# Converting the last weight matrix by column halves, with conversion slots in every chain

## The chip, the cores and the metric

The kernel runs on one core of one Trainium2 chip. The metric is device microseconds (us) of one execution, the median of several runs. Five engines work side by side from their own in-order queues: TensorE (PE: matmuls and transposes; PEld: its weight loads), VectorE (DVE), ScalarE (ACT), GpSimd (POOL) and SyncE (SP), which here issues every DMA.

## What the reference computes

Causal attention with 2 x 12 heads over 448 positions of 64, then two gated layers over the 896 tokens of width 768. Cut to what matters:

```python
x = attn_out.transpose(0, 2, 1, 3).reshape(896, 768)
h = x @ moe_w_in                      # 768 -> 2048
x = (h * sigmoid(h)) @ moe_w_out      # 2048 -> 768
h = x @ moe2_w_in                     # 768 -> 1024
sm = exp(h - max(h)) / (sum(exp(h - max(h))) + 1e-9)
solu = h * sm
ln = (solu - mean(solu)) / sqrt(var(solu) + 1e-6) * moe2_g_ln
out = ln @ moe2_w_out                 # 1024 -> 768
```

The inputs are float32, except that the four weight matrices reach the chip as 64-bit floats, as pairs of 32-bit words.

## The kernel before, in words

The work has five stages: attention, then the four matrix products. Every product is done with operands split into a high and a low part (`h`, `l`), and three matmuls for each block: high by high, high by low, low by high. So each weight chunk has to be loaded, converted from 64-bit words to float32 with integer operations, and split.

A chunk is 128 rows by 384 columns. `order` (lines 238 to 245) lists all chunks of the four matrices in the order in which they are loaded and converted; the sixteen chunks of the last one, `(4, 0)` to `(4, 15)`, stand at its end. `RAWS` = 4 loads are ahead of the conversion. For one chunk the steps are: `load_w` (L193, a DMA issued by SyncE), `conv_a` (L202, ScalarE scales the high words), `shift_w` (L217, VectorE shifts the low words), `conv_b` (L209 and L212, VectorE joins the words; between the two it shifts the next chunk), and the split. For the last matrix the split is `split4`: `high4` (L496, ScalarE: `w4h` = chunk times the gain) and `low4` (L500, VectorE: `w4l` = chunk times the gain minus `w4h`).

The stage around the change is the last one, lines 481 to 615. The 896 tokens are seven tiles of 128 (`NT` = 7). For each tile `t` there is

- `gemm3(t)` (L535 to L537): the third product, 2 x 512 columns in the PSUM tile `h`, 36 matmuls;
- `chain(t)` (L544 to L562): the softmax-like gate and the layer norm's statistics, alternating between VectorE and ScalarE. VectorE takes the maximum (L549), ScalarE the exponential (L550), VectorE divides and multiplies (L552 to L555), ScalarE squares (L557, "Square") and subtracts the mean (L558, "Identity"), VectorE and GpSimd finish (L559, L560). It has two places, `fill` and `fill2`, in which other work is put in the queues;
- `transp4(t)` (L570): eight TensorE transposes into the PSUM tiles `tp`;
- `evict4(t)` (L578 on ScalarE, L579 on VectorE): splits the transposed tile into `lh` and `ll`;
- `gemm4(t)` (L590 to L592): the fourth product. It goes over the output columns in two halves, 0 to 383 and 384 to 767 (0 to 511 and 512 to 767 for the last tile), each with its own PSUM buffer of the pool `gm`, which has two. For each half it goes over eight row blocks `k` with three matmuls each. ScalarE then evicts the half (L593) and SyncE writes it out (L594).

Everything is in a hand-written order: each engine's queue follows the order of the program's text. The loop of lines 602 to 609 does `gemm3(t)` and `chain(t)` for the seven tiles. From tile 5 on it also puts `transp4(0)` and `transp4(1)` ahead of the chain, and the chain's first place is then taken by `evict4(0)` and `evict4(1)`. The loop of lines 611 to 615 does `gemm4(t)` and, behind it, `transp4(t + 2)` and `evict4(t + 2)`.

The conversions of the last matrix are put in slots. One slot is a call of `feed4` (L508): it takes the oldest waiting chunk, issues `high4` for it, `conv_b` for the next one of the list if there is any, `low4` for the first, then `conv_a` of the one after and a load. With three chunks waiting, as at the first slot, it splits one more. There is one slot before chain 0, two in each of chains 0 to 4, and one in each of chains 5 and 6 (the second place; the first has the eviction). What is left is done by `feed_to(4, N4 - 1)` at line 610, behind chain 6.

Before the change chunk `m` holds row block `k = m // 2` and column half `n = m % 2` of the last matrix (lines 490 and 649).

Of the kernel before, what the change touches and what calls it, by code (L numbers as in the profile page):

```python
# [20 lines left out]
DM = H * D  # L21
# [4 lines left out]
KF2 = DF2 // 128  # L26
NT = T // 128
CH = 384
# [14 lines left out]
def fused(ctx, tc, qT, kT, vv, vt, w1, w2, w3, w4, gl, out):  # L43
# [18 lines left out]
    with tc.manual_schedule():  # L62
# [174 lines left out]
        N4 = KF2 * DM // CH  # L237
# [9 lines left out]
        pend = []  # L247
# [11 lines left out]
        def feed():  # L259
            m = fed[0]  # L260
            fed[0] += 1
            at = lambda a: order[a] if a < len(order) else None
            if m + 1 < len(order):
                conv_a(*order[m + 1])
            for _ in range(2):
                if len(pend) >= lag[0]:
                    finish(pend.pop(0))
            if m < len(order):
                n, c = order[m]
                conv_b(n, c, x3 if n == 3 else xs, at(m + 1))  # L270
                pend.append(m)
            if m + RAWS < len(order):
                load_w(*order[m + RAWS])

        def feed_to(n, c):
            while (n, c) not in ready:
                feed()
# [3 lines left out]
        def pair():  # L281
            t = psd.tile([128, B, 512], F32, name="h", tag="h")
            return [t[:, b] for b in range(B)]
# [49 lines left out]
        for i in range(NP2 + TL + 2):  # L333
            live = i < NP2
            n, r, p, x = i - 1, i - TL, i - TL - 1, i - TL - 2
# [61 lines left out]
        for f in range(KF):  # L397
            t = pair()
# [3 lines left out]
            for half in range(2):  # L402
# [3 lines left out]
                m = 2 * f + half + 4  # L406
# [80 lines left out]
        nc.sync.dma_start(gain, gl)  # L487

        def part4(m):
            k, n = divmod(m, 2)  # L490
            sl = slice(CH * n, CH * n + CH)
            return wx[4, m], gain[:, k:k + 1], w4h[:, k, sl], w4l[:, k, sl]

        def high4(m):
            x, g, h, _ = part4(m)
            nc.scalar.activation(h, x, AF.Copy, scale=g)  # L496

        def low4(m):
            x, g, h, l = part4(m)
            nc.vector.scalar_tensor_tensor(l, x, g, h.bitcast(F32), ALU.mult, ALU.subtract)  # L500
            wx.pop((4, m))
            ready.add((4, m))
# [5 lines left out]
        def feed4():  # L508
            m = fed[0]
            fed[0] += 1  # L510
            if len(pend) >= XS:
                split4(order[pend.pop(0)][1])
            old = order[pend.pop(0)][1] if pend else None
            if old is not None:
                high4(old)
            if m < len(order):
                conv_b(*order[m], xs, order[m + 1] if m + 1 < len(order) else None)
                pend.append(m)
            if old is not None:
                low4(old)  # L520
            if m + 1 < len(order):
                conv_a(*order[m + 1])
            if m + RAWS < len(order):
                load_w(*order[m + RAWS])
# [3 lines left out]
        def gemm3(t):  # L528
            ps = psd.tile([128, 2, 512], F32, name="h", tag="h")
            ts = slice(128 * t, 128 * t + 128)  # L530
            for n in range(2):
                for k in range(KD):
                    o = (n * KD + k) * 512
                    wh, wl = w3h[:, o:o + 512], w3l[:, o:o + 512]
                    nc.tensor.matmul(ps[:, n], yh[:, k, ts], wh, start=k == 0, stop=False)  # L535
                    nc.tensor.matmul(ps[:, n], yh[:, k, ts], wl, start=False, stop=False)  # L536
                    nc.tensor.matmul(ps[:, n], yl[:, k, ts], wh, start=False, stop=k == KD - 1)  # L537
            hps[t] = ps
# [5 lines left out]
        def chain(t, fill, fill2):  # L544
            ps = hps[t]
            s = dp.tile([128, 12], F32, name="s", tag="s", bufs=LAG + 2)
            e = dp.tile([128, 2, 512], F32, name="e", tag="e", bufs=LAG)
            col = lambda m: s[:, m:m + 1]
            nc.vector.tensor_reduce(col(0), ps, AX.XY, ALU.max, negate=True)  # L549
            nc.scalar.activation(e, ps, AF.Exp, bias=col(0), accum_out=col(1))  # L550
            fill()
            nc.vector.tensor_scalar(col(2), col(1), 1e-9, None, ALU.add)  # L552
            nc.vector.reciprocal(col(3), col(2))
            nc.vector.scalar_tensor_tensor(e, e, col(3), ps, ALU.mult, ALU.mult, accum_out=col(4))
            nc.vector.tensor_scalar(col(5), col(4), -1.0 / DF2, None, ALU.mult)  # L555
            fill2()
            nc.scalar.activation(ps, e, AF.Square, bias=col(5), accum_out=col(6))  # L557
            nc.scalar.activation(e, e, AF.Identity, bias=col(5))  # L558
            nc.vector.tensor_scalar(col(7), col(6), 1.0 / DF2, 1e-6, ALU.mult, ALU.add)  # L559
            nc.gpsimd.tensor_tensor(col(9), col(7), mhalf, ALU.pow)  # L560
            lns[t] = e
            rstd[t] = col(9)  # L562
# [3 lines left out]
        def transp4(t):  # L566
            for n in range(2):
                tp = tps[t, n] = psd.tile([128, 4, 128], F32, name="tp", tag="tp")
                for m in range(4):
                    nc.tensor.transpose(tp[:, m], lns[t][:, n, 128 * m:128 * m + 128], ident)  # L570

        def evict4(t):
            lh = dp.tile([128, KF2, 128], F32R, name="lh", tag="lh")
            ll = dp.tile([128, KF2, 128], F32R, name="ll", tag="ll")
            for n in range(2):
                tp = tps.pop((t, n))
                sl = slice(4 * n, 4 * n + 4)
                nc.scalar.activation(lh[:, sl], tp, AF.Copy)  # L578
                nc.vector.tensor_tensor(ll[:, sl], tp, lh[:, sl].bitcast(F32), ALU.subtract)  # L579
            lnt[t] = (lh, ll)  # L580
# [17 lines left out]
        def fill():  # L598
            if pend or fed[0] < len(order):
                feed4()  # L600

        for t in range(NT):
            gemm3(t)
            if t == 0:
                fill()
            z = t - NT + 2
            if z >= 0:
                transp4(z)
            chain(t, (lambda: evict4(z)) if z >= 0 else fill, fill)
        feed_to(4, N4 - 1)  # L610
        for t in range(NT):
            gemm4(t)
            if t + 2 < NT:
# [48 lines left out]
```

## Time and profile before

| what | value |
|---|---|
| three runs | 462.68, 465.28, 465.45 us; median 465.28 |
| the profiled execution, its own time | 463.06 us |
| its span from first to last instruction | 461.3 us |
| TensorE busy in the span | 444.8 us, 96% |
| VectorE, ScalarE, GpSimd busy | 322.3, 231.4, 152.9 us |
| granted TensorE clock, mean | 0.993 |

A span is measured from the first to the last instruction; what lies around it (1.76 us here) belongs to the execution's time. Busy time of TensorE is modelled from pipelined matmuls: a matmul's own duration overlaps the next one's, so distances are read from start to start. The granted clock is the share of full speed (2.4 GHz) that TensorE was given: 1.00 or 0.50, and a value between them is a stretch with both.

### The profile page before, as it was taken

What the parts mean: (1) busy time and instruction counts of PE and PEld (TensorE: products, weight loads), DVE (VectorE), ACT (ScalarE), POOL (GpSimd) and SP (SyncE); (2) the same over time, 40 slices, a digit from 0 to 9 for tenths busy, and PEclk for the clock granted to TensorE, in tenths of its full rate; (3) what the DMA queues carried; (4) which work ended last, traced back from release to release, by engine and by line L of the source; (5) the groups of instructions that cost most, each with busy time, mean ns of one, the idle gap of its engine ahead of it and who ended that gap; (6) DMA issues with size and microseconds to landing.
All of it is one profiled execution on the core that took longest, in us unless ns stands there. A gap on an engine that the chain in (4) does not pass through costs nothing.

```text
span 461.3 us, 6916 instructions
## 1 busy us (share of the span) xinstructions
PE 444.8 (96%) x2360; PEld 380.5 (82%) x2360; DVE 322.3 (70%) x720; ACT 231.4 (50%) x538; POOL 152.9 (33%) x156
## 2 busy tenths in 40 slices
PE   8899999999999999999999999999999998799997
PEld 5555555778999999999999999999888887699996
DVE  4977989759999898887695968846797767221110
ACT  4999899644433434344444334434466665321211
POOL 2312315527777566674332333323400000000000
PEclk9999999999999999999999999999999999799999
DMA  5776211204433424333754847544033300010111
GB/s 159 219 240 177 65 35 36 78 25 137 138 103 104 135 74 133 103 104 106 218 161 134 234 149 220 175 112 136 2 103 104 91 11 1 17 53 34 49 38 51
DMA packets 26386, 49.20 MB, mean 107 GB/s; under 512 B 6128, under 2 KB 13936, under 8 KB 26352
## 3 DMA queue, kind: packets, MB, share of 16 engines
q1 hardware_dynamic: 26352, 48.77, 35.7%
q8 instruction: 18, 0.29, 0.3%
q14 instruction: 16, 0.13, 0.1%
HBM read 46.01 MB, written 2.75 MB: 106 GB/s over the span
## 4 chain that ended last, share of the span: by engine, by line
PE 84%; DVE 8%; ACT 6%; issue 1%; DVEq 0%; ACTq 0%
PE h L290 7%; PE h L292 7%; PE h L291 7%; PE h L423 7%; PE h L422 7%; PE h L424 7%; PE h L537 4%; PE ps L590 4%; PE h L536 4%; PE h L535 4%; PE ps L591 4%; PE ps L592 4%; PE pv L175 4%; ACT e L126 3%; DVE e L120 3%; PE tr L149 3%
## 5 line engine op out<-in xcount | busy, mean ns | idle before, releaser
L228 POOL TENSOR_TENSOR wl<-wx,wh 128x384 fp32r<-128x384 f32 x64 | 74.7, 1168 | 100.2 <-ACT wh L227 99.0
L227 ACT ACTIVATE wh<-wx 128x384 fp32r<-128x384 f32 x64 | 33.4, 523 | 71.6 <-DVE wx L212 29.8
L202 ACT ACTIVATE wr<-wr 128x384 f32<-128x384 f32 x91 | 49.9, 554 | 33.3 <-DMA wr<-w_in 33.3
L290 PE MATMUL h<-xh,wh 128*128 128x448 f32 x180 | 65.8, 366 | 0.7 <-DVE sg L298 0.7
L212 DVE SCALAR_TENSOR_TENSOR wx<-wr,wx 128x384 uint32<-128x384 uint32 x96 | 66.4, 692 | 0.0
L291 PE MATMUL h<-xl,wh 128*128 128x448 f32 x180 | 65.7, 365 | 0.0
L292 PE MATMUL h<-xh,wl 128*128 128x448 f32 x180 | 65.7, 365 | 0.0
L217 DVE TENSOR_SCALAR wr<-wr 128x384 uint32<-128x384 uint32 x96 | 57.9, 603 | 4.0 <-DMA wr<-w_in 3.8
L209 DVE SCALAR_TENSOR_TENSOR wx<-wr 128x384 uint32<-128x384 uint32 x96 | 59.1, 615 | 1.3 <-POOL gl L300 1.3
L422 PE MATMUL h<-gh,wh 128*128 128x448 f32 x160 | 58.6, 367 | 0.0
L423 PE MATMUL h<-gl,wh 128*128 128x448 f32 x160 | 58.6, 366 | 0.0
L424 PE MATMUL h<-gh,wl 128*128 128x448 f32 x160 | 58.6, 366 | 0.0
L300 POOL TENSOR_TENSOR gl<-sg,gh 128x448 fp32r<-128x448 f32 x32 | 41.0, 1280 | 20.8 <-DVE gh L299 11.0
L126 ACT ACTIVATE e<-e,st 128x384 f32<-128x384 f32 (+3 forms) x84 | 43.3, 526 | 5.5 <-DVE st L120 5.5
L590 PE MATMUL ps<-w4h,lh 128*128 128x384 f32 (+2 forms) x112 | 39.4, 352 | 4.5 <-ACT w4h L496 4.5
L579 DVE TENSOR_TENSOR ll<-tp,lh 128x512 fp32r<-128x512 f32 x14 | 9.0, 686 | 43.4 <-ACT lh L578 43.4
L591 PE MATMUL ps<-w4l,lh 128*128 128x384 f32 (+2 forms) x112 | 38.9, 347 | 0.0
L592 PE MATMUL ps<-w4h,ll 128*128 128x384 f32 (+2 forms) x112 | 38.7, 346 | 0.0
L290 PEld LDWEIGHTS h<-xh,wh 128*128 128x128 f32 x180 | 33.8, 188 | 3.8 <-DVE sg L298 1.1
L136 POOL TENSOR_TENSOR e<-e,st 128x384 f32<-128x384 f32 x24 | 19.6, 838 | 50.1 <-ACT aT L164 34.7
L291 PEld LDWEIGHTS h<-xl,wh 128*128 128x128 f32 x180 | 33.8, 188 | 2.7
L292 PEld LDWEIGHTS h<-xh,wl 128*128 128x128 f32 x180 | 33.8, 188 | 2.7
(101 smaller groups left out, 849.8 us busy)
## 6 DMA issues: line engine op xcount, KB each, us to landing
wr<-w_in SPq DMA_DIRECT2D x96, 384.0 KB, 3.7
k<-kT_in SPq DMA_DIRECT2D x12, 224.0 KB, 3.2
q<-qT_in SPq DMA_DIRECT2D x12, 192.0 KB, 3.3
v<-vv_in SPq DMA_DIRECT2D x12, 192.0 KB, 2.9
out<-o SPq DMA_DIRECT2D x12, 192.0 KB, 1.8
qt<-qT_in SPq DMA_DIRECT2D x24, 16.0 KB, 2.8
v<-vt_in SPq DMA_DIRECT2D x12, 32.0 KB, 2.5
out<-o SPq DMA_DIRECT2D x1, 256.0 KB, 2.0
```

What stands on the lines that cost most here:

```text
L209: nc.vector.scalar_tensor_tensor(xu, high, 0x80000000, low, ALU.bitwise_and, ALU.bitwise_or)
L212: nc.vector.scalar_tensor_tensor(xu, high, 3, xu, ALU.logical_shift_left, ALU.bitwise_or)
L217: nc.vector.tensor_scalar(low, low, 29, None, ALU.logical_shift_right)
L228: (lo_engine or nc.gpsimd).tensor_tensor(l, x, h.bitcast(F32), ALU.subtract)
L290: nc.tensor.matmul(ps[:, :S], wh, rh, start=k == 0, stop=False)
L291: nc.tensor.matmul(ps[:, :S], wh, rl, start=False, stop=False)
L292: nc.tensor.matmul(ps[:, :S], wl, rh, start=False, stop=k == KD - 1)
L422: nc.tensor.matmul(ps[:, :S], wh, rh, start=f == 0, stop=False)
L423: nc.tensor.matmul(ps[:, :S], wh, rl, start=False, stop=False)
L424: nc.tensor.matmul(ps[:, :S], wl, rh, start=False, stop=f == KF - 1)
L590: nc.tensor.matmul(ps[:, :w], lh[:, k], w4h[:, k, ns], start=k == 0, stop=False)
L591: nc.tensor.matmul(ps[:, :w], lh[:, k], w4l[:, k, ns], start=False, stop=False)
```

## The change

The last matrix is laid out and converted by column halves: chunk `m` now holds row block `m % 8` of column half `m // 8`. In the chains of the last two tiles a slot is added behind the eviction in the first place, and the remainder behind the last chain becomes a loop over slots.

```diff
         def part4(m):
-            k, n = divmod(m, 2)
+            n, k = divmod(m, KF2)
             sl = slice(CH * n, CH * n + CH)
             return wx[4, m], gain[:, k:k + 1], w4h[:, k, sl], w4l[:, k, sl]
...
             z = t - NT + 2
             if z >= 0:
                 transp4(z)
-            chain(t, (lambda: evict4(z)) if z >= 0 else fill, fill)
-        feed_to(4, N4 - 1)
+            def first():
+                if z >= 0:
+                    evict4(z)
+                fill()
+
+            chain(t, first, fill)
+        while pend:
+            fill()
         for t in range(NT):
             gemm4(t)
...
-        "w4": chunks(inputs["moe2_w_out"].reshape(KF2, 128, DM).transpose(1, 0, 2)),
+        "w4": chunks(inputs["moe2_w_out"].reshape(KF2, 128, 2, CH).transpose(1, 2, 0, 3)),
```

`fill()` is one slot, if any chunk is waiting or not yet converted.

## Rows read from the trace of the kernel before

**Rows 1.** The page, busy tenths and granted clock in 40 slices of 11.53 us.

```profile
PE   8899999999999999999999999999999998799997
...
PEclk9999999999999999999999999999999999799999
```

**Rows 2.** Waits of TensorE from 380 us on: total us, times, longest us.

```profile
PE ps L590 <- ACT w4h L496: 4.5, 1, 4.5
```

**Rows 3.** TensorE in order of time: start us, us, instruction, [idle before <-releaser].

```profile
386.98 0.42 PE L590 MATMUL ps<-w4h,lh 128*128 128x384 f32 x1
...
390.60 0.34 PE L592 MATMUL ps<-w4h,ll 128*128 128x384 f32 x1
395.44 0.69 PE L590 MATMUL ps<-w4h,lh 128*128 128x384 f32 x1 [4.51 <-ACT w4h L496]
...
402.87 1.03 PE L570 MATMUL tp<-ident,e 128*128 128x128 f32 x8
403.66 0.42 PE L590 MATMUL ps<-w4h,lh 128*128 128x384 f32 x1
```

**Rows 4.** ScalarE in order of time, chains 5 and 6.

```profile
380.43 0.63 ACT L496 ACTIVATE w4h<-wx,gain 128x384 fp32r<-128x384 f32 x1
...
383.19 1.12 ACT L557 ACTIVATE h<-e,s 128x1024 f32<-128x1024 f32 x1 [1.70 <-DVE s L555]
...
389.70 0.63 ACT L496 ACTIVATE w4h<-wx,gain 128x384 fp32r<-128x384 f32 x1
392.46 1.12 ACT L557 ACTIVATE h<-e,s 128x1024 f32<-128x1024 f32 x1 [2.13 <-DVE s L555]
...
393.74 1.15 ACT L558 ACTIVATE e<-e,s 128x1024 f32<-128x1024 f32 x1
394.79 1.11 ACT L496 ACTIVATE w4h<-wx,gain 128x384 fp32r<-128x384 f32 x2
397.20 0.58 ACT L593 ACTIVATE o<-ps,s 128x384 f32<-128x384 f32 x1 [1.30 <-PE ps L592]
```

**Rows 5.** Busy time by stretch, with granted clock, DMA share and GB/s.

```profile
370.00:380.00 10.00, 10.00 (x49) 8.17 (x48) 6.44 (x15) 7.09 (x13) 0.55 (x1) 1.00 0.00 0
392.00:394.00 2.00, 0.00 (x0) 0.00 (x0) 1.93 (x7) 1.51 (x3) 0.00 (x0) 1.00 0.00 0
394.00:395.44 1.44, 0.00 (x0) 0.00 (x1) 0.10 (x3) 1.44 (x3) 0.55 (x1) 0.50 0.00 0
395.44:400.74 5.30, 5.30 (x16) 4.93 (x16) 1.13 (x2) 1.04 (x2) 0.00 (x0) 0.50 0.10 37
400.74:403.00 2.26, 2.26 (x15) 2.22 (x15) 0.00 (x0) 0.00 (x0) 0.00 (x0) 0.98 0.00 0
403.66:412.22 8.56, 8.56 (x51) 8.53 (x50) 1.29 (x2) 1.54 (x3) 0.00 (x0) 1.00 0.13 47
```

**Rows 6.** VectorE in order of time, chains 5 and 6.

```profile
383.07 0.55 DVE L209 SCALAR_TENSOR_TENSOR wx<-wr 128x384 uint32<-128x384 uint32 x1
...
384.80 0.15 DVE L559 TENSOR_SCALAR s<-s 128x1 f32<-128x1 f32 x1
386.38 1.22 DVE L549 TENSOR_REDUCE s<-h 128x1 f32<-128x1024 f32 x1 [1.44 <-PE h L537]
389.37 1.29 DVE L579 TENSOR_TENSOR ll<-tp,lh 128x512 fp32r<-128x512 f32 x2 [1.76 <-ACT lh L578]
...
390.95 1.28 DVE L554 SCALAR_TENSOR_TENSOR e<-e,s,h 128x1024 f32<-128x1024 f32 x1
...
392.34 0.55 DVE L209 SCALAR_TENSOR_TENSOR wx<-wr 128x384 uint32<-128x384 uint32 x1
...
393.40 0.61 DVE L500 SCALAR_TENSOR_TENSOR w4l<-wx,gain,w4h 128x384 fp32r<-128x384 f32 x1
393.93 0.14 DVE L559 TENSOR_SCALAR s<-s 128x1 f32<-128x1 f32 x1
395.42 1.15 DVE L500 SCALAR_TENSOR_TENSOR w4l<-wx,gain,w4h 128x384 fp32r<-128x384 f32 x2 [1.34 <-ACT w4h L496]
```

## The prediction, made blind

> **What bounds the kernel now.** I read the page's forty slices first: TensorE is at nine or ten tenths nearly everywhere, and apart from the first two slices and the last only slices 34 and 35, from 381 to 404 us (a slice is 11.53), show a lower busy share, and the second of them a lower granted clock too [rows 1]. So the end of the kernel is set by TensorE's own stream, and time can be had only where that stream stands still or runs slowly. The waits of TensorE from 380 us to the end are a single one: 4.5 us, released by ScalarE's write of `w4h` (L496) [rows 2]. In TensorE's order of time the place is exact. The third product of tile 6 ends, the eight transposes of tile 1 run, and at 386.98 the last product (`gemm4`) of tile 0 begins. Its matmuls run to the one that starts at 390.60, then nothing starts until 395.44, and the tile's product is over at 402.87, where the next transposes start [rows 3].
>
> Why there: a matmul block of row block k in column half 0 reads chunk 2k of the last matrix. Blocks k = 0 to 6 are 21 matmuls, one each 0.178 us (below), so the next is due at 390.72; it needs chunk 14. The conversions go one chunk per slot: chunks 0 and 1 in the slot before chain 0, then two in each of chains 0 to 4, so 12 of 16 (0 to 11) are done when chain 5 begins. Chains 5 and 6 have one slot each (chunk 12 at 380.43 and chunk 13 at 389.70 on ScalarE), and chunks 14 and 15 come as a pair at 394.79, behind all of chain 6 [rows 4]. TensorE resumes 0.65 us after that start.
>
> The wait has a second cost behind it. The granted clock is 1.00 until 394.00 with TensorE already idle for three us, then 0.50 (the 1.2 GHz level) until 400.74, by when matmuls have run without a gap for 5.3 us, and 0.98 after [rows 5]. The same 48 matmuls of tile 1 take 8.56 us at full clock [rows 5]; those of tile 0 took 402.87 - 386.98 = 15.89. So the stall and its slow stretch cost 15.89 - 8.56 = **7.33 us**: 395.44 - 390.72 = 4.72 of standing still, and 27 matmuls in 7.43 where 27 x 0.178 = 4.81 would do, 2.62. The Trainium skill (TensorE: Matmul & The Clock Gate, "Terms") puts the penalty of a throttled stretch at its length times one minus the granted share: here some 6.8 us at half give 3.4 (an estimate from that rule), and the sum would be 4.72 + 3.4 = 8.1 instead of 7.33. The trace disagrees by as much as the 1.44 us of the low clock that lay inside the idle time, where there was nothing to slow down; I take the rows.
>
> **The change, part by part.** *Column halves.* The chunk order, its address in memory and the slices it is written to change; the number, size and kind of loads and conversions don't. Chunks 0 to 7 are now column half 0 and 8 to 15 column half 1. Half 0 of tile 0 then needs nothing later than chunk 7, converted in chain 2. Half 1 begins 24 x 0.178 = 4.28 later, at 391.26, and its blocks need one chunk each 0.535 us: chunk 12 at 393.40, chunk 13 at 393.93, chunk 14 at 394.47, chunk 15 at 395.01. No DMA is moved past another: the loads come in the same order and the bytes per chunk are equal; from 370 to 380 us, before either chain, the DMA share is 0.00, since all chunks have landed [rows 5].
>
> *One more slot in chains 5 and 6, behind the evictions.* Chunk 12 goes to chain 5's first slot, 13 to its second, 14 and 15 to the two of chain 6, and nothing is left after it. I go through both queues with the durations of before.
>
> VectorE, chain 5. The first slot puts chunk 12's low part and chunk 14's conversion (L209, L217, L212, L500) between the eviction (L579) and L552. From L209 at 383.07 to L559 at 384.80 these four take 1.73 [rows 6]. All that follows is later by that: the Square on ScalarE goes from 383.19 to 384.92 [rows 4]. The second slot now has chunk 15, with no next chunk to shift, so no L217: three instructions, 393.93 - 392.34 = 1.59 as chain 6 shows [rows 6]. L559 then comes at 384.80 + 1.73 - 0.14 = 386.39 and ends by 386.54. The reduction of chain 6, which began at 386.38 after 1.44 us of idle time [rows 6], is late by 0.16. That idle time is what hides the 1.73; without it the whole would fall on chain 6.
>
> VectorE, chain 6. The first slot holds only chunk 14's low part, 0.53 from start to next (393.40 to 393.93 [rows 6]). So L554 moves from 390.95 by 0.16 + 0.53 to 391.64, and the second slot (chunk 15's low part alone) begins at 392.34 + 0.69 = 393.03 and ends at 393.64.
>
> ScalarE. The high parts of 14 and 15 stand behind the eviction of chain 6, at 389.70 + 0.16 = 389.86 and half a us later, done at about 390.98. They use the 2.13 us in which ScalarE waits for L555 [rows 4]. The Square moves from 392.46 to 393.15, the Identity from 393.74 to 394.43, and the instruction behind it from 394.79 to 395.48 [rows 4]. That one is now L593, the eviction of tile 0's half 0, done at 396.06.
>
> *What is late next.* Chunk 15 is whole at 393.64 and due at 395.01: 1.4 us to spare. Chunk 14: 391.35 against 394.47. `gemm4` of tile 0 ends at 386.98 + 8.56 = 395.54, the transposes of tile 2 take 403.66 - 402.87 = 0.79 [rows 3], and `gemm4` of tile 1 begins at 396.33. It needs the PSUM buffer that L593 empties at 396.06 (`gm` has two): 0.27 to spare, the thinnest margin. This wait is not in the trace of before; from below it costs 0. From above, the nearest row is the 1.34 us that a VectorE conversion there waited for ScalarE [rows 6]: one such wait in chain 6 would put L593's end at 397.40 and cost 1.07. I take 0, since L496 here starts 0.9 before VectorE comes to L500. The evictions of tile 1 (L579 at 389.37 plus 0.16, 1.29 long) are done at 390.8, long before 396.33. Chain 5's lengthening reaches nobody else: the transposes of tiles 5 and 6 stand three tiles and more later in TensorE's queue.
>
> **Sum.** 7.33 - 0 = 7.33 us less. The profiled execution took 463.06 (span 461.3 and 1.76 around it), which gives 455.73. The runs shown lie from 462.68 to 465.45 with 465.28 in the middle, 2.2 above the profiled one; nothing in the trace says where those 2.2 come from. The same 7.33 off the median gives 457.95 and off the lowest 455.35. I take the middle of 455.73 and 457.95: 456.8 us.
>
> **The rivals.** *A new wait in the old place (partial gain).* ScalarE's in-order queue keeps L593 behind chain 6, and the margin of 0.27 is within what my walk can miss. For it: the slot in chain 6 lengthens that very chain by 0.53. Against: 1.07 is the most a row supports, and so short a wait came with no lower clock (it fell only after three us of standing still [rows 5]). Time: 456.8 + 1.07 = 457.9.
>
> *The change doesn't take the wait away.* If chunk 15 still came last, with chain 6 in front of it, TensorE would stop in half 1 instead: 463 to 465, no change. Against it: the slots stand in the code before the Square, and the count of 16 chunks over the slots closes with none left.
>
> *Slower: the halves become one wait.* If `gemm4` of tile 0 waited, at its first matmul, for the last write of the whole tile `w4h`/`w4l`, it would start at 393.64 instead of 386.98: 6.66 us idle, and 2.62 for the clock again, 9.28 against 7.33 removed: 1.95 slower, 467.2 against the median. It decides from the point where the idle time passes 7.33 - 2.62 = 4.71. Against it: in the trace of before 21 matmuls ran ahead of chunk 14's write, so the waits go by region.
>
> **How the numbers follow.** Forecast (all of the stall goes) 0.85; partial 0.09; nothing taken away 0.04; one wait, slower, 0.02. A measurement of this kernel can tell about 1% from no change, 4.65 us. The first case is 1.6% and the second 1.3 to 1.6%, so I give faster 0.93 (a little off for the spread of the runs), within 1% 0.06, slower by more 0.01, as even the slower rival is only 0.4% slower. The range: from 455.35 less 0.55, since another execution's stall may have cost a little more than the profiled one's, so 454.8; up to 457.95 plus the 1.07 of the partial case, rounded up, 459.2.
>
> **What would show it.** In the profile of the changed kernel: no wait of TensorE on L496 after 380 us, at most a short one on L593; the granted clock 1.00 in every stretch from 380 us on; `gemm4` of tile 0 over in about 8.6 us; the Square of chain 5 some 1.7 us later against its reduction and that of chain 6 some 0.5; all sixteen L496 ahead of chain 6's Square. I am wrong if TensorE waits for a conversion or an eviction by more than 1 us, or if the clock falls without any wait; and wrong in the size alone if the executions spread as before and the median doesn't follow the profiled one.

## The result and the profile after

The changed kernel takes 458.26 us (median of six runs, 456.5 to 458.63), the kernel before 465.05 in the runs beside it (six, 462.68 to 466.0): a ratio of 0.9853 with a 95% interval of 0.9827 to 0.988, so 1.2 to 1.7% faster. The forecast was 456.8 in a range of 454.8 to 459.2.

The profiled execution took 458.11 us with a span of 456.3. On its page the dip of slices 34 and 35 [rows 1] is gone, from the busy tenths of TensorE and from its granted clock:

```profile
PE   8899999999999999999999999999999999999997
...
PEclk9999999999999999999999999999999999999999
```

From 330 us to the end the waits of TensorE list nothing, where the kernel before had its 4.5 us on L496 [rows 2]. In TensorE's order of time the product of tile 0 now lies without a gap between two groups of transposes (start us, us, instruction):

```profile
388.72 1.03 PE L570 MATMUL tp<-ident,e 128*128 128x128 f32 x8
389.51 0.42 PE L590 MATMUL ps<-w4h,lh 128*128 128x384 f32 x1
...
398.07 1.03 PE L570 MATMUL tp<-ident,e 128*128 128x128 f32 x8
398.86 0.42 PE L590 MATMUL ps<-w4h,lh 128*128 128x384 f32 x1
```

It takes 398.07 - 389.51 = 8.56 us, against 15.89 before [rows 3]: the 7.33 us of the forecast. That they agree to the hundredth is chance: an undisturbed product of a tile takes about 8.41 or 8.56 us in these traces (tile 1's here takes 8.41, the second row below). The two stretches: their length, the busy time of PE, PEld, DVE, ACT and POOL, then granted clock, DMA share and GB/s:

```profile
389.51:398.07 8.56, 8.56 (x51) 8.53 (x50) 4.87 (x11) 6.00 (x11) 0.75 (x2) 1.00 0.00 0
398.86:407.27 8.41, 8.41 (x52) 8.37 (x51) 1.29 (x2) 1.66 (x4) 0.00 (x0) 1.00 0.19 71
```

ScalarE's queue in chains 5 and 6 of the changed kernel shows where the conversions went:

```profile
382.96 0.62 ACT L496 ACTIVATE w4h<-wx,gain 128x384 fp32r<-128x384 f32 x1
...
383.90 0.63 ACT L496 ACTIVATE w4h<-wx,gain 128x384 fp32r<-128x384 f32 x1
387.46 1.12 ACT L557 ACTIVATE h<-e,s 128x1024 f32<-128x1024 f32 x1 [2.93 <-DVE s L555]
...
392.30 1.13 ACT L496 ACTIVATE w4h<-wx,gain 128x384 fp32r<-128x384 f32 x2
395.60 1.12 ACT L557 ACTIVATE h<-e,s 128x1024 f32<-128x1024 f32 x1 [2.16 <-DVE s L555]
...
396.87 1.15 ACT L558 ACTIVATE e<-e,s 128x1024 f32<-128x1024 f32 x1
397.93 1.03 ACT L593 ACTIVATE o<-ps,s 128x384 f32<-128x384 f32 x2
```

Chunks 12 and 13 are converted in chain 5, 14 and 15 in chain 6, all four ahead of that chain's Square (L557), where before the last pair came behind its Identity [rows 4]. What now stands behind the Identity is L593, the eviction of tile 0's first half. VectorE over the same two chains:

```profile
382.62 1.29 DVE L579 TENSOR_TENSOR ll<-tp,lh 128x512 fp32r<-128x512 f32 x2 [1.76 <-ACT lh L578]
383.83 0.55 DVE L209 SCALAR_TENSOR_TENSOR wx<-wr 128x384 uint32<-128x384 uint32 x1
...
388.93 0.15 DVE L559 TENSOR_SCALAR s<-s 128x1 f32<-128x1 f32 x1
388.99 1.22 DVE L549 TENSOR_REDUCE s<-h 128x1 f32<-128x1024 f32 x1
391.97 1.29 DVE L579 TENSOR_TENSOR ll<-tp,lh 128x512 fp32r<-128x512 f32 x2 [1.76 <-ACT lh L578]
393.18 0.61 DVE L500 SCALAR_TENSOR_TENSOR w4l<-wx,gain,w4h 128x384 fp32r<-128x384 f32 x1
...
395.48 0.61 DVE L500 SCALAR_TENSOR_TENSOR w4l<-wx,gain,w4h 128x384 fp32r<-128x384 f32 x1
```

The reduction of chain 6 (L549) no longer has idle time ahead of it; before there were 1.44 us [rows 6]. The added slot has eaten just that.

One number doesn't fit yet. The span is only 5.0 us shorter, not 7.33. The transposes of tile 1 start at 388.72 and in the kernel before at 386.19, so 2.53 us were lost earlier, in code that the change doesn't touch. From the transposes of tile 2 to the end it is 58.23 us against 58.43. So -7.33 + 2.53 - 0.20 = -5.00. The last experiment is about those 2.53.

### The profile page after: what moved, and what is told of

It reads as the page before. It is cut to its first block, busy times and chain, and to the rows that moved or that the text cites. A ratio compares the mean times of both kernels' runs of the same rounds, so it can differ in the third digit from the quotient of the medians.

```text
span 456.3 us, 6916 instructions
## 1 busy us (share of the span) xinstructions
PE 444.6 (97%) x2360; PEld 378.5 (83%) x2360; DVE 322.7 (71%) x720; ACT 231.2 (51%) x538; POOL 152.8 (33%) x156
## 4 chain that ended last, share of the span: by engine, by line
PE 86%; DVE 7%; ACT 5%; issue 1%; DVEq 0%; ACTq 0%
PE h L290 8%; PE h L292 8%; PE h L291 8%; PE h L423 7%; PE h L422 7%; PE h L424 7%; PE ps L590 4%; PE ps L591 4%; PE ps L592 4%; PE h L535 4%; PE h L537 4%; PE h L536 4%; PE pv L175 4%; ACT e L126 3%; DVE e L120 3%; PE tr L149 3%
## 5 line engine op out<-in xcount | busy, mean ns | idle before, releaser
L212 DVE SCALAR_TENSOR_TENSOR wx<-wr,wx 128x384 uint32<-128x384 uint32 x96 | 67.4, 703 | 0.0
L290 PE MATMUL h<-xh,wh 128*128 128x448 f32 x180 | 66.3, 368 | 0.7 <-DVE sg L298 0.7
L217 DVE TENSOR_SCALAR wr<-wr 128x384 uint32<-128x384 uint32 x96 | 59.3, 617 | 3.4 <-DMA wr<-w_in 2.9
L422 PE MATMUL h<-gh,wh 128*128 128x448 f32 x160 | 58.6, 366 | 0.0
L209 DVE SCALAR_TENSOR_TENSOR wx<-wr 128x384 uint32<-128x384 uint32 x96 | 57.5, 599 | 1.3 <-POOL gl L300 1.3
L590 PE MATMUL ps<-w4h,lh 128*128 128x384 f32 (+2 forms) x112 | 38.3, 342 | 0.0
L591 PE MATMUL ps<-w4l,lh 128*128 128x384 f32 (+2 forms) x112 | 37.8, 337 | 0.0
L290 PEld LDWEIGHTS h<-xh,wh 128*128 128x128 f32 x180 | 33.8, 188 | 4.3 <-DVE sg L298 1.1
```

The source lines that it names most:

```text
L209: nc.vector.scalar_tensor_tensor(xu, high, 0x80000000, low, ALU.bitwise_and, ALU.bitwise_or)
L212: nc.vector.scalar_tensor_tensor(xu, high, 3, xu, ALU.logical_shift_left, ALU.bitwise_or)
L217: nc.vector.tensor_scalar(low, low, 29, None, ALU.logical_shift_right)
L290: nc.tensor.matmul(ps[:, :S], wh, rh, start=k == 0, stop=False)
L422: nc.tensor.matmul(ps[:, :S], wh, rh, start=f == 0, stop=False)
L590: nc.tensor.matmul(ps[:, :w], lh[:, k], w4h[:, k, ns], start=k == 0, stop=False)
```

## The experiments

**Each part alone.** First the column halves with the slots of before (the two edits of `part4` and `w4`, nothing else):

```diff
-            k, n = divmod(m, 2)
+            n, k = divmod(m, KF2)
...
-        "w4": chunks(inputs["moe2_w_out"].reshape(KF2, 128, DM).transpose(1, 0, 2)),
+        "w4": chunks(inputs["moe2_w_out"].reshape(KF2, 128, 2, CH).transpose(1, 2, 0, 3)),
```

> Column halves alone, slots as before. My theory: chunks 13, 14 and 15 are converted when they were before, but needed only in half 1. Counted from the first matmul of gemm4 of tile 0: chunk 14 is due at 7.49 us, its high part is ready at 8.4 and its low part at 9.05, so TensorE waits about 1.0 us for L496 and 0.4 us for L500. gemm4 of tile 0 takes about 10.0 us (15.89 before, 8.56 after), the granted clock stays 1.00: 5.9 us of the 7.33 are saved. Rival (both parts are needed): the wait is still 3 us or more and the clock falls behind it, gemm4 of tile 0 takes 12 us or more.

Measured: 457.66 us (four runs), ratio 0.9866 (0.9843 to 0.9889). The waits of TensorE from 330 us on (total us, times, longest us):

```profile
PE ps L590 <- ACT w4h L496: 0.8, 1, 0.8
PE ps L591 <- DVE w4l L500: 0.2, 1, 0.2
```

From the end of tile 1's transposes to the start of tile 2's, with the columns of the stretches of tile products above:

```profile
387.66:397.77 10.11, 9.14 (x51) 8.24 (x50) 6.36 (x14) 6.55 (x11) 0.55 (x1) 1.00 0.00 0
```

10.11 us against 10.0 expected, at full clock: the halves alone save 15.89 - 10.11 = 5.78 of the 7.33.

Then the slots alone, with the chunks in the order of before (the edit of the chain's first place and of the loop behind it, as in the diff of the change, without the two above):

```diff
+            def first():
+                if z >= 0:
+                    evict4(z)
+                fill()
...
+            chain(t, first, fill)
+        while pend:
+            fill()
```

> Extra slots alone, chunks in the order of before. My theory: chunk 14 is due 3.74 us after the first matmul of gemm4 of tile 0; its high part is ready at 3.5, its low part at 4.4 us, so TensorE waits about 0.5 us for L500. gemm4 of tile 0 takes about 9.05 us, the clock stays 1.00: 6.8 us of the 7.33 are saved. Rival (both parts are needed): the wait is 3 us or more and the clock falls; gemm4 of tile 0 takes 12 us or more.

Measured: 456.89 us (four runs), ratio 0.9856 (0.983 to 0.9881). The one wait of TensorE from 330 us on, and the stretch of tile 0's product:

```profile
PE ps L591 <- DVE s L552: 0.2, 1, 0.2
```

```profile
387.46:396.41 8.95, 8.75 (x52) 8.39 (x50) 4.87 (x11) 6.40 (x11) 0.74 (x2) 1.00 0.00 0
```

8.95 us against 9.05 expected: 6.94 of the 7.33 are saved. (The profile puts the wait down to L552, the instruction right behind chunk 14's low part, L500; L591 reads what L500 writes.) So the rival "both parts are needed" falls. Either part alone takes most of the stall away, and their gains don't add up: 5.78 and 6.94 alone, 7.33 together. By the times alone the three kernels can't be told apart, since the intervals overlap; by the trace they can. That both parts together beat the slots alone is therefore shown only as 8.95 against 8.56 us for this one product, not in the time of the kernel.

**What the slow clock costs by itself.** In the kernel before, matmuls that nobody needs fill the wait. The extra work is only this; the output's computation is the same:

```diff
                 for k in range(KF2):
+                    if t == 0 and ns.start == 0 and k == KF2 - 1:
+                        junk = psd.tile([128, 2, 512], F32, name="h", tag="h")
+                        for _ in range(26):
+                            nc.tensor.matmul(junk[:, 0, :CH], lh[:, 0], w4h[:, 0, :CH], start=True, stop=True)
                     nc.tensor.matmul(ps[:, :w], lh[:, k], w4h[:, k, ns], start=k == 0, stop=False)
```

> The kernel before, with 26 matmuls into an unused PSUM buffer put ahead of the last row block of half 0 of tile 0, about 4.6 us of work in the 4.7 us of waiting. My theory (the slow stretch is a second cost of standing still): TensorE goes on at the same time as before, some 8.5 us after the first matmul, the granted clock stays 1.00, and gemm4 of tile 0 takes 8.56 + 4.72 = 13.3 us instead of 15.9: 2.6 us faster than before. Rival (the clock falls for another reason, or the 2.6 us belong to late conversions): the clock is 0.50 again behind it or the matmuls after it wait, and the time is that of before.

Measured: 461.71 us (seven runs), ratio 0.9955 (0.9939 to 0.9971), with 464.17 beside it: 1.3 to 2.8 us faster than before, by doing more. TensorE in order of time (lines are four further down here, L594 is L590 and L595 is L591):

```profile
391.56 4.75 PE L593 MATMUL h<-w4h,lh 128*128 128x384 f32 x26
396.23 0.44 PE L594 MATMUL ps<-w4h,lh 128*128 128x384 f32 x1
396.88 0.45 PE L595 MATMUL ps<-w4l,lh 128*128 128x384 f32 x1 [0.21 <-DVE w4l L500]
```

And the stretches around it; the granted clock, the third number from the end, is 1.00 in both:

```profile
387.00:396.00 9.00, 9.00 (x56) 8.99 (x54) 5.80 (x12) 5.40 (x9) 0.55 (x1) 1.00 0.00 0
396.00:402.00 6.00, 5.79 (x33) 5.27 (x32) 1.15 (x2) 1.48 (x4) 0.00 (x0) 1.00 0.09 33
```

TensorE resumes 8.47 us after its first matmul (at 387.76), as before (395.44 - 386.98 = 8.46), the clock stays at 1.00, and the product ends at 401.59: 13.83 us instead of 15.89. So the slow stretch costs some 2.06 us beyond the wait, not 2.62 (some, since undisturbed products differ by 0.15). Of the missing 0.56, 0.47 is seen in TensorE's rows: the matmul at 396.88 starts 0.65 after the one ahead of it and not 0.18, because chunk 14's low part isn't ready. In the kernel before the distance is the same 0.65, from 395.44 [rows 3] to

```profile
396.09 0.69 PE L591 MATMUL ps<-w4l,lh 128*128 128x384 f32 x1
```

There this wait lay partly under the slow matmul, and the prediction counted all of it as clock. The total, 7.33, is the same.

**The slower rival, made on purpose.** The changed kernel with its sixteen chunks reversed, so that the first matmul of tile 0 needs the chunk that is converted last:

```diff
-            n, k = divmod(m, KF2)
+            n, k = divmod(N4 - 1 - m, KF2)
...
-        "w4": chunks(inputs["moe2_w_out"].reshape(KF2, 128, 2, CH).transpose(1, 2, 0, 3)),
+        "w4": chunks(inputs["moe2_w_out"].reshape(KF2, 128, 2, CH)[::-1, :, ::-1].transpose(1, 2, 0, 3)),
```

> The changed kernel with its 16 chunks in reversed order, so that the first row block of half 0 needs the chunk converted last: the slower rival of the prediction, made on purpose. My theory: the first matmul starts about 4.0 us after the place where it starts in the changed kernel (L496 of chunk 15), the second another 2.5 us later (L500 of chunk 15), the clock falls during that time, and from the end of the transposes of tile 1 to the start of those of tile 2 it takes about 6.7 us of standing still, 8.6 us of matmuls and 1.6 to 2.6 us for the slow stretch, 16.9 to 17.9 us: 8.3 to 9.3 us more than the changed kernel, 1 to 2 us slower than the kernel before. Rival (a wait ahead of the product is caught up later): less than 6 us more than the changed kernel.

Measured: 465.55 us (one run) beside 464.17 of the kernel before. The waits of TensorE, and the stretches of tile 0's product:

```profile
PE ps L590 <- ACT w4h L496: 3.7, 1, 3.7
PE ps L591 <- DVE w4l L500: 2.2, 1, 2.2
```

```profile
390.00:391.50 1.50, 0.00 (x0) 0.00 (x0) 0.83 (x2) 1.50 (x5) 0.00 (x0) 1.00 0.00 0
...
392.18:394.84 2.66, 0.44 (x2) 0.19 (x2) 2.50 (x7) 0.55 (x1) 0.00 (x0) 0.69 0.00 0
...
398.20:400.00 1.80, 1.80 (x7) 1.80 (x7) 0.00 (x0) 0.00 (x0) 0.00 (x0) 0.50 0.00 0
400.00:405.50 5.50, 5.50 (x33) 5.47 (x32) 0.00 (x0) 0.58 (x1) 0.00 (x0) 1.00 0.10 36
```

TensorE stands still for 3.7 us, starts one matmul at 392.18 and waits again until 394.84. The clock falls in that third stretch, is at the 1.2 GHz level through 400.00, and back at 1.00 after. From the end of tile 1's transposes (387.42 + 0.79 = 388.21) to 405.50 it takes 17.29 us, 8.73 more than the changed kernel, within the 8.3 to 9.3 expected. Nothing of it is caught up: the order of conversions alone, with the same instructions, makes this product 17.29 - 15.89 = 1.40 us longer than in the kernel before. The times, 465.55 and 464.17, point the same way, but a single run is too few to show a loss of that size.

**What is late next.** The changed kernel with three ScalarE copies behind the Identity of chain 6 (into a free buffer that nothing reads), so that the eviction L593 comes later:

```diff
             lns[t] = e
+            if t == NT - 1:
+                junk = xs.tile([128, CH], F32, name="wx", tag="wx")
+                for _ in range(3):
+                    nc.scalar.activation(junk, w4h[:, 0, :CH].bitcast(F32), AF.Copy)
```

> The changed kernel with three extra ScalarE copies of 128x384 behind the Identity of chain 6 (they write a free buffer that nothing reads). The eviction of tile 0's half 0 (L593) then stands some 3 x 0.48 = 1.45 us later in ScalarE's queue; in the changed kernel it ends 0.35 us before the first matmul of tile 1. My theory (that eviction is what is late next): TensorE waits about 1.1 us ahead of gemm4 of tile 1, released by L593, the clock stays 1.00. Rival (there is more room than the walk says, or another buffer): no wait.

Measured: 456.88 us (one run). The one wait of TensorE from 330 us on (L594 is L590, L597 is L593 there), and ScalarE in order of time:

```profile
PE ps L594 <- ACT o L597: 1.0, 1, 1.0
```

```profile
395.67 1.62 ACT L564 ACTIVATE wx<-w4h 128x384 f32<-128x384 f32 x3
397.19 1.03 ACT L597 ACTIVATE o<-ps,s 128x384 f32<-128x384 f32 x2
```

The three copies put L593 1.52 us back; the product of tile 1, due at 396.60 behind the transposes that start at 395.81, begins at 397.81, 1.21 late and 0.04 after the end of that eviction (397.19 + 0.58). So the margin was 1.52 - 1.21 = 0.31 us. An eviction that comes later than that makes TensorE wait, at the price of its lateness and with the granted clock at 1.00. That nothing else would be late before it wasn't tried; of the margins worked out it is the thinnest.

**The place within the chain.** The changed kernel with the added slot ahead of the eviction:

```diff
             def first():
-                if z >= 0:
-                    evict4(z)
                 fill()
+                if z >= 0:
+                    evict4(z)
```

> The changed kernel with the added slot ahead of the eviction in chains 5 and 6 instead of behind it. My theory: the place within the chain does not matter; the evictions of tile 0 and tile 1 come 1.7 and 0.5 us later on VectorE, both still before their products; gemm4 of tile 0 takes 8.6 us and no wait of TensorE longer than 0.3 us appears. Rival (the place behind the evictions is what makes it work): TensorE waits 1 us or more for L579 of tile 0 or tile 1.

Measured: 457.62 us (one run), no wait of TensorE from 330 us on; tile 0's product takes 397.58 - 388.22 - 0.79 = 8.57 us. That the slot stands behind the evictions is not what makes it work.

**Where the 2.53 us went.** Both kernels once more, unchanged.

> The changed kernel once more, unchanged. In its first profile the 540 matmuls of the first product (first to last L290) took 111.8 us, 2.0 more than in the kernel before (109.8) at the same granted clock and with no wait, which hides 2.0 of the 7.33 us. Theory (the pace of that stage differs from one execution to the next): it takes 109.8 in some of the executions, and then the time is about 456 us, gemm4 of tile 0 again 8.56 us. Rival (the change itself slows the first product): 111.8 us in all of them.

> As after_again_1: 109.8 or 111.8 us for the first product by chance (theory), always 111.8 (rival). gemm4 of tile 0 takes 8.56 us.

> The kernel before once more. Theory: 109.8 or 111.8 us for the first product by chance; gemm4 of tile 0 takes 15.9 us whatever that is, if where the clock falls within the wait does not move. Rival (the spread of its runs comes from the wait): the first product takes 109.8 and gemm4 of tile 0 differs from 15.9 by 1 us or more.

Measured: 457.49, 455.54 and 463.42 us. The row of L290 (first and last start of the first product's matmuls) in four profiles: the kernel before as first shown, the changed kernel as first shown, and the changed kernel's two further executions.

```profile
L290 PE MATMUL h<-xh,wh x180: 362/365/472, 98.5 to 208.3; 128*128 128x448 f32 x180
```

```profile
L290 PE MATMUL h<-xh,wh x180: 362/368/468, 99.1 to 210.9; 128*128 128x448 f32 x180
```

```profile
L290 PE MATMUL h<-xh,wh x180: 362/368/468, 98.4 to 210.2; 128*128 128x448 f32 x180
```

```profile
L290 PE MATMUL h<-xh,wh x180: 362/365/471, 98.4 to 208.3; 128*128 128x448 f32 x180
```

The stage takes 109.8 to 109.9 us or 111.8, and one and the same kernel shows both. So the change alone doesn't make it slow. That it makes the longer stage more frequent isn't excluded: of the six profiles of kernels with both parts three have the longer one, of the five others none. Where the changed kernel has the shorter one, it takes 455.54 us; the forecast's figure for an execution like the profiled one of before was 455.73. Tile 0's product takes 8.56 and 8.42 us in the changed kernel's two further executions. The rest of the 2.53 is 0.6 at the very start (the first score matmul at 6.2 instead of 5.6 us) and rounding. The kernel before, profiled again, has the shorter stage (109.9) and 403.35 - 386.53 - 0.79 = 16.03 us for tile 0's product, so its stall is the same within 0.14 us in both profiles, and "the spread comes from the wait" finds no support in them. Two profiles are few: the mean granted clock of the kernel before is 0.993 in most of its runs, as in these two, but 0.996 in five of the fourteen beside the experiments, so the slow stretch was shorter in those (464.91, 463.06, 463.06, 464.63 and 463.84 us, spread over most of the range). What makes the stage take one time or the other wasn't found.

## Why the prediction was right, point by point

**Where and how much.** The stall was read from one wait and from the distance between two groups of transposes, compared with the next tile's. That gave 7.33 us, and the change gave 15.89 - 8.56 = 7.33 in the trace. The mechanism, a wait for late conversions with a slow stretch behind it, is shown by the filled wait and by the reversed order. What the prediction didn't ask is whether one part of the change would do; the experiments answer that either nearly does.

**How it is made up.** The forecast split it into 4.72 of standing still and 2.62 of slow clock. The second was too large by 0.56: the filled wait puts the clock at some 2.06, and most of the rest is a wait for L500 that the slow matmul partly covered. The rule of the Trainium skill (TensorE: Matmul & The Clock Gate, "Terms"), from which the prediction estimated 3.4 and a sum of 8.1, is still further off. The 1.44 us of low clock inside the idle time, to which the prediction laid the difference, is worth half of that at half speed, 0.72 of some 0.8.

**The walk through the queues.** The forecast had chain 6's reduction 0.16 late; it starts 388.99 - 388.72 = 0.27 after the transposes of tile 1, and 0.19 in the kernel before: 0.08 late. L593 was to start 395.48 - 386.98 = 8.50 us after tile 0's first matmul; it starts 397.93 - 389.51 = 8.42 after it. Chunk 15 was to be whole 1.4 us before its use: it is due at 389.51 + 8.03 = 397.54 and done at 395.48 + 0.61 = 396.09, 1.45 before. The thinnest margin was put at 0.27; it is 398.86 - 397.93 - 0.58 = 0.35 in this trace and 0.31 by the experiment. No row of before showed it, and adding up durations found it.

**The rivals.** No new wait took the old place, and the late eviction shows that the one named does come once its margin is used up. The slower rival's price, 9.28, measures 8.73 when the order is reversed, so 1.40 slower than before and not 1.95. That the waits go by region and not by tile holds: TensorE ran half 0 while half 1 was still being converted.

**The number.** 456.8 lay 1.5 us below the median, inside the range. The step at fault is the last: the middle of the profiled execution and the median was taken because nothing told where the 2.2 us between them came from. Of three profiled executions of the changed kernel two have the longer first product and took 458.11 and 457.49, one the shorter and took 455.54. All three lie 0.7 us or more from the middle, and the 7.33 taken off the median of the kernel before (457.95) would have been the better anchor for a median. The medians differ by 465.05 - 458.26 = 6.79 us, half a us less than the trace's 7.33; which of the two stage times each of these runs had isn't known.

## What to carry to other kernels

When TensorE stands still at the seam between two stages, compare a whole tile's product there with the next tile's: the difference holds the wait, the slow clock behind it and whatever hides under that, without having to split them (here to within the 0.15 us by which undisturbed tiles differ). Before adding work to a chain, look for the idle time that will take it (here 1.44 us on VectorE and 2.1 us on ScalarE), and then for the next instruction behind the chain that another engine needs. The gains of two remedies for one stall need not add up: try each alone before keeping both, and read them in the trace where the times can't tell them apart.

## What was not expected of the hardware

The first product's 540 matmuls of 448 columns take 109.8 or 111.8 us in executions of one and the same kernel, with the granted clock at 1.00 and no wait but one of 0.7 us in either: 0.2026 or 0.2066 us from start to start. Of the eleven profiled executions here, eight have the first and three the second; the second product's matmuls, of the same shape, don't follow (98.0 us from the first to the last L422 of tile `h` in the kernel before, 97.9 in the changed one). Most of the spread between runs may be this; that is argued from these profiles and not shown.

The other is that a wait filled with useless matmuls made the kernel 1.3 to 2.8 us faster, since the clock then stayed at its upper level.
